# Windowed attention before two matrix layers: a new order of TensorE's work over the two units of a head pair

## The chip, the cores and the metric

The kernel runs on one core of one Trainium2 chip. The metric is the device time of one execution in microseconds (us), the median of three runs. TensorE (PE, with its weight loads listed as PEld), VectorE (DVE), ScalarE (ACT), GpSimd (POOL) and the DMA queue of SyncE (SP) each work through their own instructions in order and wait for one another by semaphores.

## The reference, cut to what matters

Attention for 4 batches and 8 heads of dimension 64: 512 local tokens and 32 global ones. A local query sees the keys at most 32 positions away and the 32 global keys; a global query sees all 544. Two matrix layers follow on the 2176 tokens of width 512.

```python
s_ll = np.where(np.abs(pos[:, None] - pos[None, :]) <= 32, scale * q_l @ k_l.T, -1e9)
a_l = sm(np.concatenate([scale * q_l @ k_g.T, s_ll], axis=-1))
out_l = a_l @ np.concatenate([v_g, v_l])
out_g = sm(scale * q_g @ k_all.T) @ v_all
x = relu(x @ w1_in) ** 2 @ w1_out            # hidden width 2048
h = x @ w2_in
out = ((a0 + a1*h + a2*h**2 + a3*h**3) / (1 + |b0|*|h| + |b1|*h**2 + 1e-6)) @ w2_out
```

## The kernel before, in words

The order of all engines is written out by hand; nothing reorders it. Attention comes first, over 16 pairs of heads `p`, each in two units `u` of 256 queries.

- **S**, `scores(p, u)` (line 779): eight products on 64x64 tiles of the array, 16 matmul records, into `s_ps[2u]` and `s_ps[2u+1]`. DVE's `maxima` reads them, adds the mask and writes `sm` with the row maxima; ACT's `exps` (line 796) takes the exponentials and their sums; `sums`, `recip` (DVE) and `scale` (POOL, line 810) divide by the sums.
- **T**, `transp(p, u)` (lines 831 and 832): five transposes with the full 128x128 array into `tc_ps[0]` and `tc_ps[1]`; `transp_evac` (ACT, line 836) and `transp_rest` (DVE) copy them to the tiles `p1` and `p2`.
- **pv(p, u)**: first **F**, the two products with the global values (line 858, full array, 4 records), then **N**, the products with the local values (line 852, 128x64 tiles, 16 records; for `u = 1` four more at line 872). `pv_local` and `pv_global` (DVE) copy the sum from `pv_ps[u]` to `x`.
- Every second pair there is work for the global queries: **G**, `g_scores` (line 903, 128x64 tiles, into `s_ps[0]` and `s_ps[1]`), then `g_scale`, `g_exps` (ACT, lines 916 and 917) and `g_norm`; in the next iteration **GT**, `g_transp` (lines 932 and 933, also into `s_ps[0:2]`, copied by ACT).

The loop `for p in range(2, NP + 2)` is a pipeline over pairs. In an iteration TensorE does S(p,0), T(p-1,0), F and N of (p-2,1), S(p,1), T(p-1,1), F and N of (p-1,0). G stands before S(p,1) where p is odd (3 to 13), GT behind S(p,1) where p is even (2 to 14). Iterations 16 and 17 have no scores; each begins with a product of the first layer (`mm1`, line 239, full array). `pv(0, 0)` stands ahead of the loop. Rings hold four `sm` tiles, three `p1` and three `p2`. SP loads `k` and `q` three pairs ahead into four buffers and `v` for two pairs at a time into two.

The first layer follows (`mm1`, `mm2`, lines 239 and 249), and after it 48 steps `s` (`Q2` = 24 is the first of the second layer, `NQ` = 48), each of four parts `step_a` to `step_d`: TensorE forms products (line 438) and multiplies finished pieces with the output weights (`blocks`, line 465); ACT copies the banks to `temp`, DVE adds (line 663 in `step_c`, which frees the bank for `step_d`) and works out the rational function with `error`, `ratio` (line 570), `refine` (line 574), `ghigh` (ACT) and `glow` (DVE, line 533). `flush` issues ACT copies for weights of the second layer that are converted meanwhile. `depart` copies the last rows out of PSUM and starts their transfers.

Of the kernel before, what the change touches and what calls it, by code (L numbers as in the profile page):

```python
# [83 lines left out]
def body(ctx, tc, qT, kW, v, w1i, w1o, w2i, w2o, coef, out):  # L84
# [221 lines left out]
    def bank(q, i):  # L306
        return s_ps[i][:, :half(q)]

    def temp(q, i):
        return u_b[q >= Q2][i][:, :half(q)]  # L310
# [173 lines left out]
    def depart(t, part):  # L484
        for k in part_of(t, part):
            i, r = rows(t)[k], out_r[128 * k:128 * k + 128]
            if k == len(rows(t)) - 1:
                o = at("row", W0 + 7680, 512)
                act.activation(o[:, 0:256], i[:, 0:256], AF.Copy)
                dve.tensor_copy(o[:, 256:512], i[:, 256:512])  # L490
                act.dma_start(r, o)
                continue
            o = strip(LAST * NPAIR, k)[:, 0:512]
            if k % 2:
                dve.tensor_copy(o, i)
            else:
                act.activation(o, i, AF.Copy)
            sync.dma_start(r, o)
# [77 lines left out]
    def square_a(q, f):  # L576
        act.activation(strip(q, f), strip(q, f), AF.Relu)
# [7 lines left out]
    def step_a(s, tick):  # L585
        p = s - 1
        one, two = 0 <= p < Q2, Q2 <= p < NQ
        if s < NQ:
            product(s, "M1", 0)
        if one:  # L590
            if s < Q2 - 2:
                square_a(p, 0)
            act.activation(temp(s, 0), bank(s, 0), AF.Copy)
            if s >= Q2 - 2:
                square_a(p, 0)
            square_b(p, 0)
            ghigh(p, 0)
        if two:
            below(p, 0)
        if Q2 < p < NQ:  # L600
            glow(p - 1, 1)
        if two:
            linear(p, 0)
            cube(p, 0)
        tick("a", s)
        if two:
            act.activation(ew(p, 1)[0], strip(p, 1), AF.Square)
        if s < NQ and not one and s != Q2 + 1:
            act.activation(temp(s, 0), bank(s, 0), AF.Copy)
        if two:  # L610
            act.activation(ew(p, 1)[1], strip(p, 1), AF.Abs, scale=cf[:, 4:5])
            linear(p, 1)
        if s == Q2 + 1:
            act.activation(temp(s, 0), bank(s, 0), AF.Copy)
        if two:
            above(p, 0)
            below(p, 1)
            if not lagging(s):
                cube(p, 1)
            logexp(p, 0)  # L620
        groups(s, 0)

    def step_b(s, tick):
        p = s - 1
        one, two = 0 <= p < Q2, Q2 <= p < NQ
        if s < NQ:
            product(s, "M2", 1)
            product(s, "M6", 0, False)
            dve.tensor_tensor(strip(s, 0)[:, :half(s)], temp(s, 0), bank(s, 1), op=ALU.add)
            if NPAIR <= s < Q1:  # L630
                flush()
            act.activation(temp(s, 1), bank(s, 0), AF.Copy)
        if two and lagging(s):
            cube(p, 1)
        if one:
            glow(p, 0)
            square_a(p, 1)
            square_b(p, 1)
        if two:
            above(p, 1)  # L640
            error(p, 0)
            ratio(p, 0)
            logexp(p, 1)
            error(p, 1)
            refine(p, 0)
        tick("b", s)
        fetch(s + 2, 0)
        groups(s, 1)

    def step_c(s, tick):  # L650
        p = s - 1
        one, two = 0 <= p < Q2, Q2 <= p < NQ
        if s < NQ:
            product(s, "M5", 1)
            product(s, "M7", 0, False)
            act.activation(temp(s, 2), bank(s, 0), AF.Copy)  # L656
        if two:
            ghigh(p, 0)
        behind = s in (Q2 + 1, Q2 + 3) or s % NPAIR in (0, NPAIR - 1)
        if two and not behind:  # L660
            ratio(p, 1)
        if s < NQ:
            dve.tensor_tensor(strip(s, 1)[:, half(s):], temp(s, 2), bank(s, 1), op=ALU.add)  # L663
        if two and behind:
            ratio(p, 1)
        if one and s < Q2:
            ghigh(p, 1)
        if two:
            glow(p, 0)
            refine(p, 1)  # L670
        tick("c", s)
        fetch(s + 2, 1)
        groups(s, 2)
# [70 lines left out]
    v_r = Ring("v", ATT2, VC, 2, VC)  # L744
    sm_r = Ring("sm", ATT2 + 2 * VC, 640, 4, 2 * KW, 2)
    p1_r = Ring("p1", ATT2 + 2 * VC + 2560, 640, 3, 2, 320)
    q_r = Ring("q", END - 4 * (QC + KC), QC, 4, QC)
    k_r = Ring("k", END - 4 * KC, KC, 4, KC)

# [89 lines left out]
    def transp_rest(p, u):  # L839
        dve.tensor_copy(pT[p, u][1], tc_ps[1][:, 0:128])  # L840

    def pv(p, u):

        v = vt[p // 2]
        c = pgT[p // 2][1]
        p1, p2 = pT.pop((p, u))
        bank = pv_ps[u]

        def win(w, o0, o1, stop=False):
            for j in range(2):  # L850
                jj = 2 * (p % 2) + j
                pe.matmul(bank[64 * j:64 * j + 64, o0:o1], v[:, VW * w + 64 * jj:VW * w + 64 * jj + 64],  # L852
                          p1[:, j, o0 + (32 if o0 >= 128 else 0):o1 + (32 if o0 >= 128 else 0)],
                          start=False, stop=stop, skip_group_check=True)

        def glob(i):
            o = VG + 256 * (p % 2) + 128 * i
            pe.matmul(bank[:, 160 * i:160 * i + 128], v[:, o:o + 128], p2, start=i == 0, stop=False,  # L858
                      skip_group_check=True)


        glob(0)
        glob(1)
        win(4 * u, 64, 160)
        win(4 * u + 1, 0, 64)
        win(4 * u + 2, 128, 224)
        win(4 * u + 3, 224, 288, stop=u == 0)
        if u:
            for j in range(2):
                jj = 2 * (p % 2) + j  # L870
                o = VE + 64 * jj
                pe.matmul(bank[64 * j:64 * j + 64, 128:160], v[:, o:o + 64], c[:, 32 * jj:32 * jj + 32],
                          start=False, stop=True, skip_group_check=True)

    def pv_local(p, half):
        b, hp = divmod(p, 4)
# [61 lines left out]
    with tc.manual_schedule():  # L938
# [110 lines left out]
        exps(1, 1, 0)  # L1049
        exps(1, 1, 1)  # L1050
        g_norm(1)
        pv(0, 0)
        for p in range(2, NP + 2):
            if p + 3 < NP:
                load_qk(p + 3)
# [13 lines left out]
            def step(*k):  # L1069
                for c in cv:  # L1070
                    w_float(*c, k)

            if cur:
                sm_tiles(p, 0)
                scores(p, 0)
                maxima(p, 0, 0)
                exps(p, 0, 0)
            else:
                mm1(p - NP)
            pv_local(p - 2, 0)  # L1080
            if pre:
                sums(p - 1, 1)
            if cur:
                maxima(p, 0, 1)
            if pre:
                norm(p - 1, 1)
                p_tiles(p - 1, 0)
                p_tiles(p - 1, 1)
                g_copies(p - 1, 0)
                g_copies(p - 1, 1)  # L1090
            step(0)
            pv_global(p - 2, 0)
            step(1)
            if pre:
                transp(p - 1, 0)
                transp_evac(p - 1, 0)
                transp_rest(p - 1, 0)
            idle(middles, p)
            step(2)
            if cur:  # L1100
                exps(p, 0, 1)
            pv(p - 2, 1)
            if odd:
                g_scores(g)
            if cur:
                sm_tiles(p, 1)
                scores(p, 1)
                if odd:
                    g_scale(g)
                    idle(waits, p)  # L1110
                    g_exps(g)
                    transp(p - 1, 1)
                    transp_evac(p - 1, 1)
                maxima(p, 1, 0)
                sums(p, 0)
                norm(p, 0)
                exps(p, 1, 0)
                maxima(p, 1, 1)
            if odd:
                g_norm(g)  # L1120
            for c in cv:
                w_split(*c, dve)
                f = w_rest(*c, True)
                if f is not None:
                    keeps.append((c[2], f))
            if p % 2 == 0 and p < NP:
                g_transp(g)
            pv_local(p - 2, 1)
            pv_global(p - 2, 1)
            if pre:  # L1130
                if not odd:
                    transp(p - 1, 1)
                    transp_evac(p - 1, 1)
                transp_rest(p - 1, 1)
            idle(ends, p)
            if cur:
                exps(p, 1, 1)
            if pre:
                pv(p - 1, 0)
            for c in slots.get(p + 1, []):  # L1140
                w_scale(*c)
            if p >= NP:
                ew1(p - NP)
        act.activation(nf[:, 0:4], cf[:, 0:4], AF.Copy, scale=-1.0)
        act.activation(nf[:, 5:6], cf[:, 5:6], AF.Abs)

# [505 lines left out]
```

## Time and profile before

| | |
|---|---|
| median of 3 runs | 835.6 us (835.46 to 836.48) |
| the profiled execution | 835.83 us, its span 834.0 us |
| granted TensorE clock | 1.00 over the whole span |
| PE busy | 827.3 us (99%) |
| DVE, ACT, POOL busy | 710.5, 637.4, 187.8 us |

A row of the timeline gives the start and the busy time of some instructions with one form. TensorE's matmuls overlap, so its busy share says little; the distance from the start of one group to the start of the next is what the group costs.

### The profile page before, as it was taken

How to read it: one execution, taken by the hardware profiler on the slowest of the kernel's cores; microseconds unless marked ns; L12 is line 12 of the kernel's file. 1: busy time of each engine (PE TensorE's matmuls, PEld its weight loads, DVE VectorE, ACT ScalarE, POOL GpSimd, SP SyncE). 2: the span in 40 equal slices, each digit the busy share in tenths (PEclk: the TensorE clock that was granted, in tenths of full speed). 3: DMA queues.
4: the chain of work that ended last, by engine and by line, in shares of the span. 5: the costliest groups of instructions: out<-in, count | busy, mean ns of one | idle time of the engine just before them, and what ended most of it. 6: DMA issues, size and time to landing. Idle time of an engine off the chain costs nothing.

```text
span 834.0 us, 15576 instructions
## 1 busy us (share of the span) xinstructions
PE 827.3 (99%) x5671; PEld 741.7 (89%) x5671; DVE 710.5 (85%) x1425; ACT 637.4 (76%) x1244; POOL 187.8 (23%) x352
## 2 busy tenths in 40 slices
PE   9999999999999999999999999999999999999997
PEld 5888888888899999999999999999999999998995
DVE  5788889997787477687788699999999999989997
ACT  6899868875677576776777787878887878888775
POOL 4677766550000111111111121111111101111100
PEclk9999999999999999999999999999999999999999
DMA  9797569934598789999986574334364344465401
GB/s 343 283 327 260 220 240 418 411 118 152 202 330 303 264 250 407 307 315 369 373 264 192 148 240 120 120 114 120 122 189 118 122 114 117 126 214 150 139 15 64
DMA packets 50445, 181.38 MB, mean 217 GB/s; under 512 B 5696, under 2 KB 8000, under 8 KB 49472
## 3 DMA queue, kind: packets, MB, share of 16 engines
q1 hardware_dynamic: 31264, 100.94, 32.1%
q0 software_dynamic: 18960, 79.18, 31.1%
q8 instruction: 45, 0.74, 0.3%
q14 instruction: 32, 0.26, 0.1%
q10 hardware_dynamic: 144, 0.26, 0.1%
HBM read 139.73 MB, written 40.63 MB: 216 GB/s over the span
## 4 chain that ended last, share of the span: by engine, by line
PE 90%; DVE 8%; ACT 1%; DMA 1%; issue 0%; SPq 0%; ACTq 0%
PE s L438 32%; PE tc L465 14%; PE pv L465 13%; PE s L465 8%; PE s L239 5%; PE pv L852 3%; PE tc L249 3%; PE pv L249 3%; PE s L779 3%; PE tc L831 3%; PE pv L858 2%; DVE x L557 1%; DVE x L553 1%; DVE e L566 1%; PE s L903 1%; DVE x L570 1%
## 5 line engine op out<-in xcount | busy, mean ns | idle before, releaser
L438 PE MATMUL s<-sh,got 128*128 128x320 f32 (+2 forms) x1120 | 279.1, 314 | 0.2 <-DVE x L663 0.2
L438 PEld LDWEIGHTS s<-sh,got 128*128 128x128 f32 x1120 | 196.8, 189 | 4.0 <-DVE x L663 0.8
L416 POOL DMA_DIRECT2D got<-pr x120 | 65.0, 542 | 535.7 <-PE s L438 455.3
L438 PE MATMUL s<-sl,got 128*128 128x320 f32 (+2 forms) x560 | 176.0, 314 | 0.0
L465 PE MATMUL tc<-g,w 128*128 128x512 f32 (+1 forms) x480 | 126.9, 383 | 0.1
L465 PE MATMUL pv<-g,w 128*128 128x512 f32 (+1 forms) x480 | 126.5, 382 | 0.0
L438 PEld LDWEIGHTS s<-sl,got 128*128 128x128 f32 x560 | 105.7, 189 | 2.4
L465 PEld LDWEIGHTS s<-g,w 128*128 128x128 f32 x576 | 93.6, 188 | 10.9
L465 PE MATMUL s<-g,w 128*128 128x256 f32 x576 | 98.8, 280 | 0.0
L465 PEld LDWEIGHTS tc<-g,w 128*128 128x128 f32 x480 | 83.2, 188 | 9.4 <-DVE g L533 0.8
L465 PEld LDWEIGHTS pv<-g,w 128*128 128x128 f32 x480 | 83.3, 188 | 8.4
L529 ACT ACTIVATE g<-x 128x512 fp32r<-128x512 f32 (+2 forms) x95 | 69.7, 734 | 14.8 <-DVE x L574 12.8
L533 DVE TENSOR_TENSOR g<-x,g 128x512 fp32r<-128x512 f32 (+2 forms) x95 | 78.0, 821 | 1.0 <-ACT g L529 0.9
L810 POOL TENSOR_SCALAR sm<-sm,rs 128x160 f32<-128x160 f32 x128 | 55.4, 457 | 30.0 <-DVE x L886 19.6
L796 ACT ACTIVATE sm<-sm,nm 128x160 f32<-128x160 f32 x128 | 55.6, 446 | 7.7 <-DVE nm L788 7.2
L549 DVE SCALAR_TENSOR_TENSOR e<-e,nf,e 128x768 f32<-128x768 f32 (+1 forms) x48 | 46.7, 973 | 9.3 <-ACT e L541 9.3
L656 ACT ACTIVATE u<-s 128x256 f32<-128x256 f32 (+2 forms) x48 | 21.0, 437 | 41.9 <-PE s L438 41.8
L788 DVE CUSTOM_DVE_ANT_0 sm<-s,mask 128x160 f32<-128x160 f32 x128 | 36.1, 322 | 15.8 <-PE s L779 13.7
L194 POOL TENSOR_TENSOR w<-cv,w 128x512 fp32r<-128x512 f32 x32 | 42.2, 1320 | 30.9 <-ACT w L188 22.7
L682 ACT ACTIVATE x<-s 128x256 f32<-128x256 f32 (+2 forms) x48 | 21.0, 438 | 35.0 <-PE s L438 33.2
L545 ACT ACTIVATE x<-x,nf 128x768 f32<-128x768 f32 (+1 forms) x48 | 47.1, 982 | 0.0
L557 DVE SCALAR_TENSOR_TENSOR x<-x,nf 128x768 f32<-128x768 f32 (+1 forms) x48 | 46.7, 973 | 0.4
(203 smaller groups left out, 1782.5 us busy)
## 6 DMA issues: line engine op xcount, KB each, us to landing
got<-pr POOLq DMA_DIRECT2D x80, 512.0 KB, 4.0
got<-pr POOLq DMA_DIRECT2D x40, 768.0 KB, 4.8
pr<-half SPq DMA_DIRECT2D x24, 512.0 KB, 5.7
v<-in_v_dram SPq DMA_DIRECT2D x7, 1408.0 KB, 8.5
k<-in_kW_dram SPq DMA_DIRECT2D x15, 592.0 KB, 6.0
r<-in_w1i_dram SPq DMA_DIRECT2D x16, 512.0 KB, 9.8
r<-in_w1o_dram SPq DMA_DIRECT2D x16, 512.0 KB, 10.8
pr<-tw SPq DMA_DIRECT2D x16, 512.0 KB, 3.4
```

The source lines that it names most:

```text
L194: pool.tensor_tensor(w[:, 1], f, w[:, 0].bitcast(F32), op=ALU.subtract)
L249: pe.matmul(acc_bank[d][:, :n], w[:, half, 128 * d:128 * d + 128], src[:, :n], start=start, stop=stop)
L416: pool.dma_start(got[q % 2][k], pairs[q >= Q2][q % NPAIR][:, o0:o1])
L438: pe.matmul(bank(q, i), a[:, k], b[:, k], start=first and k == 0 and j == 0, stop=k == 1 and j == 2, skip_group_check=True)
L465: pe.matmul(dst, a, b, start=first and j == 0, stop=j == KF - 1 and final, skip_group_check=True)
L529: act.activation(gpair(q, f)[0], strip(q, 2 + f), AF.Copy)
L533: eng.tensor_tensor(gl, strip(q, 2 + f), gh.bitcast(F32), op=ALU.subtract)
L545: act.activation(t, h, AF.Identity, scale=nf[:, 3:4], bias=nf[:, 2:3])
L549: dve.scalar_tensor_tensor(a, in0=a, scalar=nf[:, 5:6], in1=b, op0=ALU.mult, op1=ALU.add)
L557: dve.scalar_tensor_tensor(t, in0=t, scalar=nf[:, 1:2], in1=h, op0=ALU.add, op1=ALU.mult)
L796: act.activation(e, e, AF.Exp, scale=-1.0, bias=nm[:, k:k + 1], accum_out=tot[:, k:k + 1])
L810: pool.tensor_scalar(e, e, rs[:, k:k + 1], 1.0, op0=ALU.mult, op1=ALU.mult)
```

## The change

The loop's order becomes: S(p,0), S(p,1), T(p-1,0), F(p-2,0), then GT or G where there is one, N(p-2,0), N(p-2,1), F(p-2,1), T(p-1,1). Both units of `pv` now belong to pair p-2, so `pv(0, 0)` leaves the prologue and iteration 17 has two. `exps(p,1,1)` moves from the end of iteration p to the head of p+1, behind `transp_evac(p-1,1)`, which moves there too with `transp_rest`, `pv_local` and `pv_global` of unit 1. The p1 and p2 rings get a fourth buffer each in space that attention leaves unused. Products are the same in number and size.

Elsewhere: `depart` copies its last row tile with one ACT copy in place of half on ACT and half on DVE; `step_a` calls `flush` ahead of a copy in steps 8 to 15; `step_b` swaps `refine(p,0)` and `error(p,1)` in step 40; `step_c` puts `ratio(p,1)` behind the addition of line 663 where s % 8 is 5, and behind `glow(p,0)` in step 40.

```diff
             if k == len(rows(t)) - 1:
                 o = at("row", W0 + 7680, 512)
-                act.activation(o[:, 0:256], i[:, 0:256], AF.Copy)
-                dve.tensor_copy(o[:, 256:512], i[:, 256:512])
+                act.activation(o, i, AF.Copy)
...
             if s < Q2 - 2:
                 square_a(p, 0)
+            if NPAIR <= s < Q1:
+                flush()
             act.activation(temp(s, 0), bank(s, 0), AF.Copy)
...
-            error(p, 1)
-            refine(p, 0)
+            if s == NQ - NPAIR:
+                refine(p, 0)
+                error(p, 1)
+            else:
+                error(p, 1)
+                refine(p, 0)
...
-        behind = s in (Q2 + 1, Q2 + 3) or s % NPAIR in (0, NPAIR - 1)
+        behind = s in (Q2 + 1, Q2 + 3) or s % NPAIR in (0, 5, NPAIR - 1)
+        first = s == NQ - NPAIR
...
-        if two and behind:
+        if two and behind and not first:
             ratio(p, 1)
...
             glow(p, 0)
+            if first:
+                ratio(p, 1)
             refine(p, 1)
...
+    p1_r.all.append(at("p1", RAW + 512, 2, 320))
+    p2_r.all.append(at("p2", RAW + 1152, 128))
...
-    def pv(p, u):
+    def pv_far(p, u):
+        v = vt[p // 2]
+        bank = pv_ps[u]
+        for i in range(2):
+            o = VG + 256 * (p % 2) + 128 * i
+            pe.matmul(bank[:, 160 * i:160 * i + 128], v[:, o:o + 128], pT[p, u][1], start=u == i == 0,
+                      stop=u == i == 1, skip_group_check=True)
+    def pv_near(p, u):
...
-        win(4 * u, 64, 160)
+        win(4 * u, 64, 160, start=u == 1)
...
+            if p > 2:
+                transp_evac(p - 2, 1)
+                transp_rest(p - 2, 1)
+                pv_local(p - 3, 1)
+                pv_global(p - 3, 1)
             if cur:
+                for u in range(2):
+                    sm_tiles(p, u)
+                    scores(p, u)
             else:
                 mm1(p - NP)
+            if pre and p > 2:
+                exps(p - 1, 1, 1)
+            if cur:
+                for j in range(2):
+                    maxima(p, 0, j)
+                    exps(p, 0, j)
             if pre:
...
                 g_copies(p - 1, 0)
                 g_copies(p - 1, 1)
+                sums(p - 1, 1)
+                norm(p - 1, 1)
                 transp(p - 1, 0)
                 transp_evac(p - 1, 0)
+            step(0)
+            if cur:
+                maxima(p, 1, 0)
+                maxima(p, 1, 1)
+            if pre:
                 transp_rest(p - 1, 0)
+            step(1)
+            pv_far(p - 2, 0)
+            if p % 2 == 0 and cur:
+                g_transp(g)
             if odd:
                 g_scores(g)
+                g_scale(g)
+                idle(waits, p)
+                g_exps(g)
+            pv_near(p - 2, 0)
             if cur:
                 sums(p, 0)
                 norm(p, 0)
                 exps(p, 1, 0)
+            pv_near(p - 2, 1)
+            step(2)
+            pv_local(p - 2, 0)
+            pv_global(p - 2, 0)
...
+            pv_far(p - 2, 1)
             if pre:
+                transp(p - 1, 1)
+            idle(middles, p)
+            if odd:
+                g_norm(g)
             idle(ends, p)
```

## Rows read from the trace of the kernel before

**Rows 1.** Windows, iterations 2 to 15: stretch, length, busy us (instructions) of PE, PEld, DVE, ACT, POOL.
```profile
17.89:104.02 86.13, 86.13 (x1290) 70.75 (x1287) 69.55 (x407) 78.09 (x304) 61.56 (x150) 1.00 0.74 278
```

**Rows 2.** Timeline of TensorE, iterations 10 and 11: start us, busy us.
```profile
67.43 0.77 PE L779 MATMUL s<-k,q 64*64 64x160 f32 x16
68.13 0.74 PE L831 MATMUL tc<-ident,sm 128*128 128x128 f32 x4
68.71 0.27 PE L832 MATMUL tc<-ident,sm 128*128 128x128 f32 x1
68.82 0.61 PE L858 MATMUL pv<-p,v 128*128 128x128 f32 x4
69.36 0.78 PE L852 MATMUL pv<-p,v 128*64 128x96 f32 x16
69.97 0.26 PE L872 MATMUL pv<-pl,v 128*64 128x32 f32 x4
70.16 0.77 PE L779 MATMUL s<-k,q 64*64 64x160 f32 x16
70.86 0.66 PE L932 MATMUL s<-ident,gs 128*128 128x128 f32 x4
...
71.47 0.64 PE L831 MATMUL tc<-ident,sm 128*128 128x128 f32 x4
71.94 0.27 PE L832 MATMUL tc<-ident,sm 128*128 128x128 f32 x1
...
73.30 0.77 PE L779 MATMUL s<-k,q 64*64 64x160 f32 x16
...
75.85 0.26 PE L872 MATMUL pv<-pl,v 128*64 128x32 f32 x4
75.94 1.17 PE L903 MATMUL s<-k,q 128*64 128x512 f32 x8
77.04 0.78 PE L779 MATMUL s<-k,q 64*64 64x160 f32 x16
77.75 0.96 PE L831 MATMUL tc<-ident,sm 128*128 128x128 f32 x4
78.54 0.27 PE L832 MATMUL tc<-ident,sm 128*128 128x128 f32 x1
...
79.90 0.37 PE L779 MATMUL s<-k,q 64*64 64x160 f32 x4
```

**Rows 3.** Timeline of TensorE in the prologue: a transpose ahead of scores.
```profile
12.17 0.27 PE L832 MATMUL tc<-ident,sm 128*128 128x128 f32 x1
12.37 0.77 PE L779 MATMUL s<-k,q 64*64 64x160 f32 x16
```

**Rows 4.** Timeline of TensorE: first scores of iteration 3, then iteration 16.
```profile
23.95 0.37 PE L779 MATMUL s<-k,q 64*64 64x160 f32 x4
...
104.02 0.50 PE L239 MATMUL s<-xh,w 128*128 128x512 f32 x1
...
108.80 0.74 PE L831 MATMUL tc<-ident,sm 128*128 128x128 f32 x4
109.38 0.27 PE L832 MATMUL tc<-ident,sm 128*128 128x128 f32 x1
```

**Rows 5.** Timeline of ACT in the prologue: the last of `g_exps(1)`.
```profile
17.18 0.30 ACT L917 ACTIVATE gs<-s,gm 128x64 f32<-128x64 f32 x1
```

**Rows 6.** Waits of weight loads after attention, 160 us to the end: total, times, longest.
```profile
PEld s L438 <- DVE x L663: 0.8, 2, 0.5
PEld tc L465 <- DVE g L533: 0.8, 2, 0.6
```

**Rows 7.** Timeline of ACT and DVE at the end of the span.
```profile
828.21 0.60 ACT L497 ACTIVATE x<-pv 128x512 f32<-128x512 f32 x1 [0.20 <-PE pv L465]
...
829.59 0.38 ACT L489 ACTIVATE row<-s 128x256 f32<-128x256 f32 x1 [0.77 <-PE s L465]
830.00 0.42 DVE L490 COPY row<-s 128x256 f32<-128x256 f32 x1 [0.40 <-ACT row L489]
```

More of the change, by code (lines that the diff above doesn't have):

```diff
@@ L840, in transp_rest, with win @@
         dve.tensor_copy(pT[p, u][1], tc_ps[1][:, 0:128])
-    def pv(p, u):
+    def pv_far(p, u):
[6 more added lines that the diff above has]
+    def pv_near(p, u):
         v = vt[p // 2]
         c = pgT[p // 2][1]
-        p1, p2 = pT.pop((p, u))
+        p1 = pT[p, u][0]
         bank = pv_ps[u]
-        def win(w, o0, o1, stop=False):
+        def win(w, o0, o1, start=False, stop=False):
             for j in range(2):
@@ L853, in win @@
                           p1[:, j, o0 + (32 if o0 >= 128 else 0):o1 + (32 if o0 >= 128 else 0)],
[L854 to L863, printed above, removed]
-        win(4 * u, 64, 160)
+                          start=start, stop=stop, skip_group_check=True)
+        win(4 * u, 64, 160, start=u == 1)
         win(4 * u + 1, 0, 64)
@@ L872, in pv @@
                 pe.matmul(bank[64 * j:64 * j + 64, 128:160], v[:, o:o + 64], c[:, 32 * jj:32 * jj + 32],
-                          start=False, stop=True, skip_group_check=True)
+                          start=False, stop=False, skip_group_check=True)
     def pv_local(p, half):
@@ L1051, in body @@
         g_norm(1)
-        pv(0, 0)
         for p in range(2, NP + 2):
@@ L1071, in step @@
                     w_float(*c, k)
+            if p > 2:
[3 more added lines that the diff above has]
+                pv_global(p - 3, 1)
             if cur:
[L1074 to L1077, printed above, removed]
+                for u in range(2):
+                    sm_tiles(p, u)
+                    scores(p, u)
             else:
                 mm1(p - NP)
-            pv_local(p - 2, 0)
-            if pre:
[L1082 to L1086, printed above, removed]
+            if pre and p > 2:
[4 more added lines that the diff above has]
+                    exps(p, 0, j)
+            if pre:
                 p_tiles(p - 1, 0)
@@ L1090, in body @@
                 g_copies(p - 1, 1)
[L1091 to L1094, printed above, removed]
+                sums(p - 1, 1)
+                norm(p - 1, 1)
                 transp(p - 1, 0)
                 transp_evac(p - 1, 0)
-                transp_rest(p - 1, 0)
[L1098 to L1102, printed above, removed]
+            step(0)
[3 more added lines that the diff above has]
+            if pre:
+                transp_rest(p - 1, 0)
+            step(1)
+            pv_far(p - 2, 0)
+            if p % 2 == 0 and cur:
+                g_transp(g)
             if odd:
                 g_scores(g)
+                g_scale(g)
+                idle(waits, p)
+                g_exps(g)
+            pv_near(p - 2, 0)
             if cur:
[L1106 to L1114, printed above, removed]
                 sums(p, 0)
@@ L1117, in body @@
                 exps(p, 1, 0)
-                maxima(p, 1, 1)
-            if odd:
-                g_norm(g)
+            pv_near(p - 2, 1)
+            step(2)
+            pv_local(p - 2, 0)
+            pv_global(p - 2, 0)
             for c in cv:
@@ L1125, in body @@
                     keeps.append((c[2], f))
[L1126 to L1129, printed above, removed]
+            pv_far(p - 2, 1)
             if pre:
[L1131 to L1134, printed above, removed]
+                transp(p - 1, 1)
+            idle(middles, p)
+            if odd:
+                g_norm(g)
             idle(ends, p)
[L1136 to L1139, printed above, removed]
             for c in slots.get(p + 1, []):
@@ L1143, in body @@
                 ew1(p - NP)
+        pv_local(NP - 1, 1)
+        pv_global(NP - 1, 1)
         act.activation(nf[:, 0:4], cf[:, 0:4], AF.Copy, scale=-1.0)
```

## The prediction

> **What bounds the kernel now.** I read the granted clock first (full speed throughout), then the busy table, the chain of waits, and the windows and timelines of the stages. In the attention loop the window shows TensorE without a gap: 86.13 of 86.13 us [rows 1]. DVE has 16.6 us to spare there, ACT 8.0 and POOL 24.6. So the stage ends when TensorE's list ends, and the question is what each group on it costs from start to start, which the timeline gives [rows 2].
>
> The same group costs different amounts by its neighbour. L832 takes 0.11 us ahead of F (68.71 to 68.82) but 0.20 ahead of scores [rows 2, 3]: leaving the full array for tiles costs 0.09. L872 takes 0.09 ahead of G, which uses the same tiles, and 0.19 ahead of S [rows 2]: 0.10. F takes 0.54 for four records that would be 0.44 at 0.11 each: 0.10. On the other side, the four big transposes take 0.58 behind S and 0.47 behind GT [rows 2], and 0.58 behind N as well [rows 4]: entering the full array costs 0.11. GT behind S takes 0.61 for five at 0.11: 0.06. What is paid is a change between the array's shapes (64x64 for S, 128x64 for N and G, full for T, GT and F); L933, with 64 columns but among full-array transposes, shows no such price, 0.61 in all.
>
> Two prices stand in no row. Leaving S I set at 0.10, as the three others. Entering S or N lies between 0 and the 0.11 of T; I take 0.05, nearest to GT's 0.06. So S to T is 0.21, N to F or T 0.21, F to N 0.15, N to S 0.15, T to S 0.14, S to GT 0.16, G to S 0.15, N to G 0.
>
> L933 loads 64 columns among full-array transposes, and 70.86 to 71.94 shows no price for it on either side beyond the 0.06 [rows 2]. So behind GT, N still pays the full array's 0.15. The Trainium skill, TensorEngine Tiling (Array Packing), Available Configurations and Key Properties, lists 128x64 as a mode of its own and says that changing the mode drains the engine. If that held for L933, N behind it would be free, 0.15 less in seven even iterations, and the result below 1.0 us lower; the rows speak against it.
>
> **The loop.** Before, an iteration has six changes. Odd: S to T twice, F to N twice, G to S, N to S, 0.42 + 0.30 + 0.30 = 1.02 us. Even: one S to T becomes S to GT, 0.97. The new order has four in either: S to T, then F (or GT, or G behind F) to N, N to F, T to S, 0.21 + 0.15 + 0.21 + 0.14 = 0.71. An odd iteration saves 0.31 and an even one 0.26; iterations 3 to 15 save 7 x 0.31 + 6 x 0.26 = 3.73 us. With the unknown entries at 0 or 0.11 it is 2.3 or 5.2.
>
> **Waits inside the loop.** In iteration 11 the transposes take 0.79 instead of 0.58 [rows 2]: they wait for POOL's scaling. An undisturbed even iteration is 5.87, an odd one 6.60 - 0.21 = 6.39, and iteration 15, without G, 6.39 - 1.10 + 0.10 = 5.39 [rows 2]. Six, six and one make 78.95, but iteration 3 to the end of 15 took 104.02 - 23.95 = 80.07 [rows 4]. So such waits cost 1.12 in all. In the new order T(p-1,1) is the last group of its iteration, and its scaling can begin once `exps(p-1,1,1)` is done near the head; T(p-1,0) was scaled an iteration earlier. I take off all 1.12; nothing less than 0 is left if I am wrong.
>
> **The two ends.** `pv(0, 0)` filled the time in which ACT ran `g_exps(1)`, which must free two score banks before S(2,0). That ends at 17.48 [rows 5], so S(2,0) starts at about 17.53; with 5.87 - 0.26 for iteration 2, S(3,0) starts at 23.14 instead of 23.95 [rows 4], 0.81 earlier. But the work of that half, F 0.44 and N 0.61 - 0.05, comes back in iterations 16 and 17: +1.00, net +0.19. In those two, products of the full array stood behind N three times (4 x 0.21 + 3 x 0.15 = 1.29 with T behind N, less 0.15 that iteration 15 already counts). Now they stand behind T and F, which have their shape: 2 x 0.21 + 2 x 0.15 = 0.72, less 0.14 counted. Saved 0.56. Attention together: -3.73 - 1.12 + 0.19 - 0.56 = -5.22.
>
> **What is moved past the queues.** ACT: `transp_evac(p-2,1)` and `exps(p-1,1,1)` now head an iteration. T(p-1,0) needs that evacuation, and only two S lie between T(p-2,1) and it: 0.70 + 0.70 less one change of 0.15, 1.25 us. Behind the six exponentials come `transp_evac(p-1,0)` and `g_exps`, which frees the banks for the next S. ACT had 78.09 us of work in iterations 2 to 15 [rows 1], and these would now take some 80.7 (17.53 to 98.2). It fits, with 2.6 to spare; I add 0.3 for small waits, bounds 0 and the next rival. DVE's 69.55 and POOL's 61.56 leave more. The fourth `p1` and `p2` keep `g_copies` from waiting for N. On SP the load of `v` now waits for F(p-3,1) at the end of iteration p-1, before for N in its first half; its first reader stands two iterations later, about 11 us, so it stays hidden. The writes of converted weights on SP wait for DVE in iteration 16 as before, and the first layer's loads stand behind them; if these came a microsecond later against TensorE, the first layer would have to wait for weights. I price that at 0, bound 1.0.
>
> **The small places.** Line 663 frees the bank that `step_d` needs; weight loads wait for it twice, 0.8 us in all, and twice for `glow`, 0.8, of which 0.6 in step 40 [rows 6]. The first two are in steps 29 and 37 (s % 8 = 5), where `ratio(p,1)` now goes behind: nothing follows it on DVE that TensorE needs sooner, because `glow(p,0)` keeps its place. In step 40 `refine(p,0)` and `glow(p,0)` move ahead of two DVE operations that nobody waits for yet. A load that waits would have run a little ahead of its product, so TensorE gains less than 1.4: I take 1.1, bounds 0.5 and 1.4. The swap in step 45 and the earlier `flush` meet no such wait: 0 (the flush delays an ACT copy by one operation that has a product's time to spare; bound +0.3). At the end the DVE half waited for the ACT half, 830.00 to 830.42 [rows 7]; one ACT copy of 512 columns takes 0.60, so it ends at 830.19: -0.23.
>
> **The sum.** -5.22 + 0.3 - 1.1 - 0.23 = -6.25 us from the profiled 835.83: 829.6. The median of the runs is 0.23 below the profiled execution, so 829.4.
>
> **The rivals.**
> 1. ACT takes over as the bound. For it: it has least to spare of the three. Against it: its idle time before (8.0 us [rows 1]) is mostly waiting for TensorE and DVE. If half of these waits stay, the loop takes 78.1 + 4.0 = 82.1 instead of 80.7 and the result is 830.8; if all stay, 834.8. I expect up to 832.
> 2. Weight loads wait for the products in flight whatever the order, so that changes of shape cost nothing of their own. TensorE: Matmul & The Clock Gate, Part 3 (What overlaps and what doesn't), of the Trainium skill has a rule of this kind: loads overlap with running matmuls only if their row groups differ. The trace speaks against it: T to T and T to F, all with 128 rows, run 0.11 apart [rows 2]. Then the 3.73 and the 0.56 fall away: 833.7.
> 3. Slower: the turnaround of `tc_ps`. If `transp_evac(p-1,1)` sits behind late exponentials on ACT, T(p,0) stalls although S covers 1.25 us. The saving, 6.25 over 14 iterations, is 0.45 an iteration; the change loses from the point at which the evacuation ends 1.7 us after an iteration's start. With 2.2 us it would be 829.4 + 14 x 0.95 = 842.7. ACT's spare time speaks against it.
> 4. Entering S and N costs as much as entering T (0.11 in place of 0.05): the loop saves 5.2 in place of 3.73, 827.9.
>
> **Chances.** Forecast 0.65, ACT bound 0.18, no price of shapes 0.04, turnaround 0.04, dearer entries 0.09. The forecast's own range is 828.4 to 830.4. For 8 in 10 I go to 827.9 below and 832.2 above. Faster by over 0.2% (1.7 us, about what a measurement of this kernel can tell): 0.95; within it 0.01; slower 0.04.
>
> **What would show it.** S(p,0) to the next S(p,0) at 5.6 in even and 6.1 in odd iterations; `mm1(0)` near 98.2 instead of 104.02; no transposes over 0.6; S and T next to each other at 0.14; no wait at line 663 in steps 29 and 37. Wrong would be gaps of PEld ahead of T that end with ACT, or an ACT busy without a break.

## The result, and the profile after

The changed kernel takes 828.99 us (median of 6 runs, 828.76 to 829.79) against 835.84 us (median of 6 runs, 835.46 to 836.48; the first three of them gave the 835.6 of the table before): 0.9919 of the time, with a 95% interval of 0.9910 to 0.9929. The forecast was 829.4. The profiled execution took 829.79, the longest of the six, and has a span of 828.0 us; that of the kernel before had 834.0. The 6.0 us between the two spans is what the rows below have to explain; between the medians it is 6.85. The repeat in experiment 6, whose profile lies at the median of its runs, has a span of 827.3 us.

The busy times on the page of the changed kernel:

```profile
PE 821.2 (99%) x5671; PEld 740.1 (89%) x5671; DVE 714.1 (86%) x1424; ACT 636.3 (77%) x1244; POOL 187.8 (23%) x352
```

TensorE is busy for 99% of the span, as before. So the time was not won from gaps that the page shows; it was won inside TensorE's groups, in changes of shape and in waits that the page counts as busy. The windows view of iterations 2 to 15 answers to [rows 1], with the same columns:

```profile
17.29:98.72 81.43, 81.43 (x1288) 69.51 (x1289) 71.45 (x405) 77.23 (x303) 62.73 (x151) 1.00 0.81 299
```

The stretch is 81.43 us long where it was 86.13, again with TensorE busy for all of it and the granted clock at full. ACT does 77.23 us of work in it: 4.2 us are left to it, where there were 8.0.

The timeline of TensorE in iterations 10 and 11 of the changed kernel (start, busy) answers to [rows 2]:

```profile
64.78 1.32 PE L789 MATMUL s<-k,q 64*64 64x160 f32 x32
66.03 0.74 PE L841 MATMUL tc<-ident,sm 128*128 128x128 f32 x4
66.61 0.27 PE L842 MATMUL tc<-ident,sm 128*128 128x128 f32 x1
66.72 0.61 PE L857 MATMUL pv<-p,v 128*128 128x128 f32 x4
67.17 0.60 PE L941 MATMUL s<-ident,gs 128*128 128x128 f32 x4
67.61 0.27 PE L942 MATMUL s<-ident,gs 128*64 128x128 f32 x1
67.81 1.35 PE L869 MATMUL pv<-p,v 128*64 128x96 f32 x32
68.98 0.26 PE L881 MATMUL pv<-pl,v 128*64 128x32 f32 x4
69.17 0.71 PE L857 MATMUL pv<-p,v 128*128 128x128 f32 x4
69.72 0.64 PE L841 MATMUL tc<-ident,sm 128*128 128x128 f32 x4
70.20 0.27 PE L842 MATMUL tc<-ident,sm 128*128 128x128 f32 x1
70.40 1.32 PE L789 MATMUL s<-k,q 64*64 64x160 f32 x32
...
73.90 1.30 PE L869 MATMUL pv<-p,v 128*64 128x96 f32 x32
75.03 0.26 PE L881 MATMUL pv<-pl,v 128*64 128x32 f32 x4
...
76.44 1.32 PE L789 MATMUL s<-k,q 64*64 64x160 f32 x32
```

Read starts, not busy times. The even iteration lasts 70.40 - 64.78 = 5.62 us and the odd one 76.44 - 70.40 = 6.04. L842 takes 0.11 ahead of F (66.61 to 66.72) and 0.20 ahead of scores (70.20 to 70.40). The transposes behind F take 0.48 (69.72 to 70.20), behind S 0.58; F takes 0.55 behind N (69.17 to 69.72) and 0.45 behind T. So T is as long as its undisturbed forms in [rows 2]. Single weight loads of T still wait 0.2 us for POOL, but no transpose starts later for it.

The attention's ends on TensorE answer to [rows 4]: the scores of iterations 2 and 3, the first layer's product at the head of iteration 16, and the first one behind the loop. The last row is that same product in the kernel before:

```profile
17.18 1.60 PE L789 MATMUL s<-k,q 64*64 64x160 f32 x32 [0.79 <-ACT gs L925]
...
23.07 1.18 PE L789 MATMUL s<-k,q 64*64 64x160 f32 x28
...
98.61 0.48 PE L239 MATMUL s<-xh,w 128*128 128x512 f32 x1
...
110.16 0.48 PE L239 MATMUL s<-xh,w 128*128 128x512 f32 x1
```

```profile
114.93 0.50 PE L239 MATMUL s<-xh,w 128*128 128x512 f32 x1
```

Iteration 16 begins at 98.61 where it began at 104.02, and the product behind the loop at 110.16 instead of 114.93: the attention gives 4.77 us. From there to the end of the span it is 717.84 us against 719.07, another 1.23. Together they are the 6.0 us of the two spans.

The waits of weight loads from 160 us to the end (total, times, longest) answer to [rows 6]; the whole list is:

```profile
PEld tc L465 <- ACT g L737: 0.6, 1, 0.6
PEld s L438 <- ACT u L633: 0.5, 2, 0.3
PEld tc L465 <- DVE g L732: 0.4, 1, 0.4
PEld tc L465 <- DVE g L532: 0.4, 2, 0.2
PEld tc L465 <- ACT x L264: 0.3, 1, 0.3
PEld s L438 <- ACT u L661: 0.2, 1, 0.2
```

The 0.8 us for line 663 (now 669) are gone, and the 0.8 for `glow` (line 533, now 532) are 0.4. The timeline of DVE in step 29 shows how: the addition at line 669, which frees the bank, now starts ahead of `ratio(p,1)` at line 569.

```profile
542.48 0.55 DVE L669 TENSOR_TENSOR x<-u,s 128x384 f32<-128x384 f32 x1
542.95 1.01 DVE L569 SCALAR_TENSOR_TENSOR x<-x,nf,e 128x768 f32<-128x768 f32 x1
```

The end of the span on ACT answers to [rows 7]: one copy of 512 columns in place of two halves on two engines, and the issue of the last row behind it. The last line is the issue in the kernel before:

```profile
823.55 0.60 ACT L489 ACTIVATE row<-s 128x512 f32<-128x512 f32 x1 [0.76 <-PE s L465]
824.18 0.37 ACTq L490 DMA_DIRECT2D out_dram<-row  x1
```

```profile
830.46 0.37 ACTq L491 DMA_DIRECT2D out_dram<-row  x1
```

From the copy's start to the issue it is 0.63 us; before it was 830.46 - 829.59 = 0.87. From the copy's start to the end of the span, though, it is 828.0 - 823.55 = 4.45 us where it was 834.0 - 829.59 = 4.41: the end does not come sooner.

### The profile page after: what moved, and what is told of

The parts are those of the page before. It is cut to its first block, busy times and chain, and to the rows that moved or that the text cites. A ratio compares the mean times of both kernels' runs of the same rounds, so it can differ in the third digit from the quotient of the medians.

```text
span 828.0 us, 15576 instructions
## 1 busy us (share of the span) xinstructions
PE 821.2 (99%) x5671; PEld 740.1 (89%) x5671; DVE 714.1 (86%) x1424; ACT 636.3 (77%) x1244; POOL 187.8 (23%) x352
## 4 chain that ended last, share of the span: by engine, by line
PE 95%; DVE 3%; DMA 1%; ACT 1%; issue 0%; SPq 0%; ACTq 0%
PE s L438 35%; PE tc L465 15%; PE pv L465 15%; PE s L465 9%; PE s L239 5%; PE tc L249 3%; PE pv L249 3%; PE pv L869 2%; PE s L789 2%; PE tc L841 2%; PE pv L857 2%; PE s L912 1%; DMA k<-in_kW_dram 1%; DVE x L556 0%; PE tc L842 0%; PE s L941 0%
## 5 line engine op out<-in xcount | busy, mean ns | idle before, releaser
L669 DVE TENSOR_TENSOR x<-u,s 128x256 f32<-128x256 f32 (+2 forms) x48 | 23.2, 483 | 26.5 <-ACT u L661 26.5
## 6 DMA issues: line engine op xcount, KB each, us to landing
r<-in_w1o_dram SPq DMA_DIRECT2D x16, 512.0 KB, 11.1
```

## The experiments

Seven kernels ran beside the kernel before, which had medians of 835.51 us (21 runs) in the series of experiments 1 to 4 and 835.3 us (18 runs) in that of 5 to 7.

**1. The order alone.** The small places (the order of DVE in steps 29, 37, 40 and 45, the `flush`, the last row) go back to their old form.

```diff
-                act.activation(o, i, AF.Copy)
+                act.activation(o[:, 0:256], i[:, 0:256], AF.Copy)
+                dve.tensor_copy(o[:, 256:512], i[:, 256:512])
...
-            if NPAIR <= s < Q1:
-                flush()
...
-        behind = s in (Q2 + 1, Q2 + 3) or s % NPAIR in (0, 5, NPAIR - 1)
+        behind = s in (Q2 + 1, Q2 + 3) or s % NPAIR in (0, NPAIR - 1)
...
```

> The new order of the attention loop alone; the edits in depart, step_a, step_b and step_c are undone. Theory (the loop is worth its changes of array shape and its lost transpose waits, the small places 1.3 us): 830.3 us, between 829.9 and 830.7, and the waits at the addition in step_c come back at steps 29 and 37. Rival (the small places are worth nothing, the loop is worth all): 829.0.

Measured: 830.48 us (830.06 to 830.84), 0.9938 of the kernel before (0.9926 to 0.9951). The order alone gives 5.0 us. The waits of its weight loads after attention are those of [rows 6] again, line 663 with 0.8 and line 533 with 0.8.

**2. The small places alone.** The kernel before, with the other half of the change.

```diff
...
-        behind = s in (Q2 + 1, Q2 + 3) or s % NPAIR in (0, NPAIR - 1)
+        behind = s in (Q2 + 1, Q2 + 3) or s % NPAIR in (0, 5, NPAIR - 1)
+        first = s == NQ - NPAIR
...
```

> The kernel before with the edits in depart, step_a, step_b and step_c alone. Theory: 1.3 us below the kernel before, 834.5, the two waits for the addition in step_c gone, and the last row's transfer issued 0.2 us sooner after its matmul. Rival (they only move time to a later wait): 835.6 or more.

Measured: 834.48 us (833.84 to 835.17), 0.9988 (0.9979 to 0.9996), 1.0 us less. Its list of waits has no line for the addition any more. The two parts of the change add up: 5.0 + 1.0 against 6.2 (experiment 6 beside its series) to 6.85 (the result) for the whole, a remainder within the spread of the runs.

**3. Two more changes of shape.** F for unit 1 goes between the N groups of the two units, so that N is split. All instructions stay; only their order and the place of the start flag differ (unit 1's sums are here never cleared, so this kernel serves for its time alone).

```diff
-        win(4 * u, 64, 160, start=u == 1)
+        win(4 * u, 64, 160, start=False)
...
+            pv_far(p - 2, 1)
             pv_near(p - 2, 1)
             step(2)
...
-            pv_far(p - 2, 1)
```

> The changed kernel with the global products of unit 1 put between the local products of unit 0 and unit 1. The same matmuls, but six changes of array shape an iteration in place of four: one more of 0.15 (full to 128x64) and one more of 0.21 (128x64 to full). Theory (TensorE pays for the changes): 16 iterations at 0.36, 5.8 us more, 834.7 us. Rival 2 (loads wait for products in flight whatever the order; the gain came from lost waits): 829.0, no difference. Rival 1 (ACT is the bound): less than half of 5.8.

Measured: 834.40 us (833.99 to 834.97), 0.9986 (0.9977 to 0.9995): 5.4 us more than the 828.99 of the changed kernel, and 5.0 more than experiment 4, which has the new order too and ran in this series. The timeline of TensorE in its iteration 10:

```profile
66.76 1.32 PE L789 MATMUL s<-k,q 64*64 64x160 f32 x32
...
69.78 0.78 PE L869 MATMUL pv<-p,v 128*64 128x96 f32 x16
70.50 0.71 PE L857 MATMUL pv<-p,v 128*128 128x128 f32 x4
71.14 0.78 PE L869 MATMUL pv<-p,v 128*64 128x96 f32 x16
71.75 0.26 PE L881 MATMUL pv<-pl,v 128*64 128x32 f32 x4
71.94 0.75 PE L841 MATMUL tc<-ident,sm 128*128 128x128 f32 x4
72.72 1.32 PE L789 MATMUL s<-k,q 64*64 64x160 f32 x32
```

The iteration lasts 5.96 us instead of 5.62. F between two N groups takes 0.64 (70.50 to 71.14), where behind N and ahead of T it took 0.55. The same instructions in another order cost 0.34 more, and none of these rows has a wait beside it: the change of shape has a price of its own. It stands where the prediction put it: N, now in two parts, takes 0.16 more (0.72 + 0.80 against 1.36, line 881 included), F between them 0.09, and T, now behind N, 0.10. The 5.0 to 5.4 us are as much as the order gained in experiment 1.

**4. Values of pairs 2 and 3 later.** In the profiled execution of the changed kernel iteration 3 lasted 29.81 - 23.07 = 6.74 us instead of the 6.04 of other odd ones. The timeline of TensorE there:

```profile
25.55 1.34 PE L912 MATMUL s<-k,q 128*64 128x512 f32 x5
26.57 0.33 PE L869 MATMUL pv<-p,v 128*64 128x96 f32 x2
26.73 0.65 PE L912 MATMUL s<-k,q 128*64 128x512 f32 x2
```

G stops after five of its eight records. They read the keys of pairs 4 and 5. SP issued the load of pair 5's keys at 15.06; the load of the values of pairs 2 and 3, `load_v(1)`, went ahead of it at 12.43. The DMA view gives that one load 11.1 us to landing, so the keys were there at about 26.1, behind the start of G at 25.55, and G's next weight loads start just behind that:

```profile
26.25 0.35 PEld L912 LDWEIGHTS s<-k,q 128*64 128x64 f32 x4 [0.51 <-issue]
```

The wait is put down to "issue" because the profile names no engine that was waited for.

In the kernel before, they landed at 25.6 as well, but G began at 26.59. The new order starts G 1.0 us sooner, ahead of its keys.

```diff
-        load_v(1)
...
             if p + 3 < NP:
                 load_qk(p + 3)
+            if p == 2:
+                load_v(1)
```

> The changed kernel with the load of the second group of values put behind the load of keys and queries of pair 5. In the changed kernel the global scores of iteration 3 start, stop for about 0.7 us and go on. Theory (they wait for the keys of pair 5, which share the bandwidth with those values): the stop goes, 828.3 us. Rival (the values then come late for iteration 4, or the stop has another cause): 829.0 or more.

Measured: 829.38 us (828.52 to 829.49), 0.9923 (0.9911 to 0.9935). In the timeline of TensorE in its profile the stop is gone: G takes 1.03 us in one group and iteration 3 lasts 6.04.

```profile
25.02 1.19 PE L912 MATMUL s<-k,q 128*64 128x512 f32 x8
26.05 1.30 PE L869 MATMUL pv<-p,v 128*64 128x96 f32 x32
```

The same load was issued at 13.31 here and landed 9.3 us later, at 22.6, well ahead of G. The other profiles of the new order bear the cause out. There, with the load order unedited, the keys landed at 25.1 to 26.4: in experiments 1, 5 and 6 up to 0.6 behind the start of G, as above (stops of 0.16, 0.66 and 0.37), in 3 and 7 ahead of it (no stop). So the stop is a wait for the keys, and its size varies with the execution. The time is not lower than that of the changed kernel, against what was expected: the profile is of the shortest of the five runs, the other four were 829.0 to 829.5, and why they gained nothing stays open.

**5. More work for ACT.** `transp_evac(p-1,0)` is issued twice, 15 copies of 0.47 us, 7.1 us in all; results do not change.

```diff
                 transp_evac(p - 1, 0)
+                transp_evac(p - 1, 0)
```

> The changed kernel with the ACT copy of the transposes of (p-1,0) done twice, 15 copies of 0.47 us from start to start more on ACT, 7.1 us. In iterations 2 to 15 of the changed kernel ACT was busy 77.2 of 81.4 us. Theory (TensorE is the bound and ACT has 4.2 us to spare, most of it usable): between 0 and 2.9 us more, 829.0 to 831.9. Rival 1 (ACT had already taken over): all 7.1 us, 836. Rival 3 (the turnaround of the transpose banks is what TensorE waits for): more than 3 us, with gaps of the weight loads ahead of the transposes that end with ACT's copy.

Measured: 832.95 us (832.44 to 833.73), 0.9972 (0.9962 to 0.9982), 3.8 us more than the changed kernel. The windows view of its iterations 2 to 15:

```profile
17.30:101.55 84.25, 83.44 (x1288) 70.92 (x1288) 71.86 (x405) 83.66 (x317) 62.67 (x152) 1.00 0.78 288
```

Its waits of weight loads from 14 to 110 us:

```profile
PEld s L789 <- ACT gs L925: 1.9, 6, 1.0
PEld tc L841 <- POOL sm L820: 1.5, 5, 0.6
```

The stage grows from 81.43 to 84.25 us, and ACT now works 83.66 of them: it sets the pace. The first line is the scores' wait for `g_exps`, six times where the changed kernel has it once, in iteration 2. Of the 83.66 - 77.23 = 6.4 us that ACT does more in this stage, 2.8 lengthened it, so 3.6 of the 4.2 us of idle time could be used. Nearly all of the rest of the 3.8 lies in iteration 16, where the last transposes take 0.84 more and their weight loads wait for POOL's scaling (0.6, the longest of the second line). In the changed kernel ACT was close to being the bound and was not it. The upper end of the expectation, 831.9, was too low by a microsecond.

**6. The changed kernel again.** No edit, in the series of experiments 5 to 7.

> The changed kernel itself, on the same chip as the other two of this call and as a mark for the earlier load order: 829.0 us, between 828.6 and 829.5 by the spread of its runs. If the stop of the global scores in iteration 3 is in most of its executions, its profile shows it again; if not, the profile lies near 826.7 to 827.3 in span.

Measured: 829.12 us (828.84 to 829.84), 0.9928 (0.9916 to 0.9941). In its profile iteration 2 starts at 16.86 (17.18 above) and iteration 3 lasts 29.16 - 22.75 = 6.41: the stop costs 0.37 here and 0.70 above. The product behind the loop starts at 109.52, and from there to the end of the span it is 717.8: against the kernel before, the attention gives 5.41 us here and the rest 1.3.

**7. Three changes of shape.** In even iterations and the last, all work of the full array (both units' T and F, and GT) stands in one block behind S, and N ends the iteration. DVE's and ACT's orders are adapted; the core of the edit:

```diff
...
+            if three:
+                pv_far(p - 2, 1)
+                transp(p - 1, 1)
...
-            pv_far(p - 2, 1)
+            if not three:
+                pv_far(p - 2, 1, first=False)
...
```

> The changed kernel with both transposes of an iteration in one stretch of full-array work where no global scores stand: in even iterations and in 15 the order is S(p,0), S(p,1), T(p-1,0), F(p-2,0), GT, F(p-2,1), T(p-1,1), N(p-2,0), N(p-2,1). N to F (0.21) and T to S (0.14) go, N to S (0.15) comes: three changes in place of four. Theory: 8 iterations at 0.20, 1.6 us less, 827.4 us. Rival (the second transposes, now 1.5 us sooner, wait for POOL's scaling or for ACT to empty the transpose bank): 829.0 or more, with gaps of the weight loads ahead of those transposes.

Measured: 834.23 us (833.61 to 834.99), 0.9986 (0.9977 to 0.9995): 5.1 us more than the changed kernel in the same series (experiment 6). Its even iteration 10 lasts 72.53 - 66.46 = 6.07 us instead of 5.62, and the waits of weight loads from 14 to 110 us say why:

```profile
PEld tc L841 <- POOL sm L820: 3.7, 16, 0.4
...
PEld s L942 <- DVE nm L798: 2.3, 7, 0.4
```

In the changed kernel the first of these lines has 1.6 us in 7 waits, none over 0.2, and the second is absent. T behind F takes 0.85 us in this iteration 10 instead of 0.48, and GT 0.69 instead of 0.44 ahead of its last transpose. One change of shape less was worth less than the distance between producer and reader that it took away. No version was found that beats the changed kernel by more than the runs' spread.

## Why the prediction was right

The forecast of 829.4 us lies 0.4 above the measured median of 828.99, which is within the narrow range (828.4 to 830.4). The mechanism, prices of shapes and waits of T, is what the rows and experiments show. That the sum came so close is in part luck. The 0.3 us for ACT and the 0.23 for the last row came to nothing, and a stop of 0.70 stood in no term; these partly cancel, and the profiled execution, at 829.79, is the longest of its six.

**Prices of shapes.** Right. Two S take 66.03 - 64.78 = 1.25 us as predicted, the iterations 5.62 and 6.04 (5.61 and 6.08). Experiment 3 tests the price by itself: about 32 more changes, expected to cost 5.8 us, cost 5.0 to 5.4, and 0.34 to 0.36 an iteration where 0.36 was expected. The entry of N, taken at 0.05 without a row, now has one: N's 32 records take 1.13 behind G (73.90 to 75.03), which uses the same tiles, and 1.17 behind GT (67.81 to 68.98), so 0.04. With the unknown entries at 0 or 0.11 the prediction's own prices give 2.4 or 5.3 for the loop, 0.1 more than it has; nothing hangs on that.

**L933.** The rows were the better guide. N behind the transpose of line 942 (before, 933) starts 0.20 later (67.61 to 67.81), where L842 ahead of F takes 0.11. N still pays for leaving the full array, although a load of 64 columns stands just ahead of it. By the prediction's other reading, which counts line 942 as the 128x64 mode of the Trainium skill, TensorEngine Tiling (Array Packing), Available Configurations and Key Properties, it would have been free.

**The loop.** Iteration 3 to the end of 15 took 98.61 - 23.07 = 75.54 us. Forecast were 80.07 - 3.73 - 1.12 + 0.3, and 0.20 less for iteration 15, whose N no longer stands ahead of a product of the first layer (part of the 0.56): 75.32. Two errors inside nearly cancel. Without the 0.70 that iteration 3 lost the loop would have taken 74.84, against 75.02 without the 0.3 for small waits on ACT: the odd iterations are 0.04 shorter than forecast and those waits did not come. In their place stands a stop that the prediction had at nothing: it did not ask whether the keys would be there for a G that starts 1.0 us sooner (experiment 4). So 0.3 too much and 0.70 too little were in the sum, and the closeness of 75.54 to 75.32 is luck in that part. The 1.12 us of T's waits for POOL is gone, as taken: in iterations 2 to 15 no T takes more than 0.59 behind S or 0.48 behind F, while weight loads still wait for its scaling seven times, 0.2 us each.

**The ends.** S(3,0) starts 0.88 us earlier (23.95 to 23.07; forecast 0.81). The way there was another: S(2,0) starts at 17.18 and not at 17.53, as soon as line 925 has left the first bank, and the two S of iteration 2 then take 18.70 - 17.18 = 1.52 instead of 1.25. Iterations 16 and 17 take 110.16 - 98.61 = 11.55 us, where before they took 114.93 - 104.02 = 10.91: +0.64, which is the 1.00 of the moved half less the remaining 0.36 of the 0.56. Attention as a whole gave 0.88 + 4.53 - 0.64 = 4.77 of the 4.92 (5.22 less 0.3) forecast.

**The small places.** They were costed at 1.1 us for the waits and 0.23 for the last row, 1.33 in all. Experiment 2 measures 1.0 (0.3 to 1.8 by its interval), and the stretch behind the attention is 1.23 shorter in the profile. The waits are all of it: of the listed ones, 0.8 us for the addition and 0.4 for `glow` are gone. The 0.23 for the last row came to nothing. The prediction ended its sum at the copy, and the issue does come 0.24 sooner behind the copy's start; but the transfer then took 828.0 - 824.18 = 3.82 us to the end of the span, 834.0 - 830.46 = 3.54 before. From the copy's start to the end of the span it is 4.4 to 4.5 us in all nine profiles, in the two with halves (before, experiment 1) as in the seven with one copy.

**The rivals.** ACT as the bound: its spare time fell to 4.2 us (forecast 2.6), and only in iteration 2 do the changed kernel's scores wait for it longer than 0.2 us, a wait that the forecast had (17.18 for 17.53). Experiment 5 shows that the rival was near: another 7.1 us of work bring it. Loads waiting for products in flight, so that shapes cost nothing: experiment 3 has the same instructions, and its forecast by that rival, 829.0, missed by 5.4. T to F, all of 128 rows, follow 0.11 us apart (66.61 to 66.72), and the weight loads of F begin together with the last transpose in front of it, here in iteration 3:

```profile
24.90 0.53 PEld L857 LDWEIGHTS pv<-p,v 128*128 128x128 f32 x4
24.90 0.27 PE L842 MATMUL tc<-ident,sm 128*128 128x128 f32 x1
```

The rule in TensorE: Matmul & The Clock Gate, Part 3 (What overlaps and what doesn't), of the Trainium skill, that loads overlap with running products only where the row groups differ, is not what these rows show.

The turnaround of `tc_ps`: in the changed kernel no wait of T for its evacuation appears, and T stays at 0.48 and 0.58. Dearer entries: 16 scores take 0.70 with one entry and one leaving, so two S would take 1.40 - 0.10 - 0.11 = 1.19 if entering cost 0.11, and 1.25 at 0.05. The rows have 1.25. For the time, this rival and the forecast lay 1.5 us apart, and 828.99 is nearer to the forecast by 0.7 only; it is the rows that decide.

## What to carry to other kernels

Where TensorE has no gap, its list can still be shortened: compare the start-to-start time of the same group behind different neighbours, and count changes of shape per iteration. Group what has one shape across two units, as long as each reader stays far enough behind its producer; experiment 7 passed that point. A reader that a new order moves forward may also meet its own load: the stop in iteration 3 is such a case. A step saved at the very end counts only if the end of the span moves with it. Before giving a neighbouring engine more to do, or its work a later place, double one of its instructions: that tells how much of its idle time is really spare.

## What the runs showed of the hardware that was not expected

- While G waited for its keys in iteration 3, the records of N's products (L869) lie between those of G's (L912): 25.55 G, 26.57 N, 26.73 G. A later group's products appear in the records before the waiting group has ended, although TensorE was described as working through its instructions in order. What that is in the engine was not tried.
- The stop cost 0.70 us in one execution and 0.37 in another of the same kernel. The head of the loop started at 17.18 and 16.86 in these two, and at 16.65 in the one of experiment 4. It moved with the first transfers: a load of keys issued at 3.05 in all three landed at 9.5, 9.2 and 8.8. Why these transfers vary was not tried.
- From the issue of the last row's transfer to the end of the span it is 3.8 us in all seven profiles with one copy, and 3.5 to 3.6 in both with two halves, for the same row. What takes the 0.25 us was not tried.
